# Windowed attention, LayerNorm and a ReLU MLP on one core: from wanted times for a list scheduler to an order written down as a permutation

## The chip, the cores and the metric

One core of one Trainium2 chip runs the whole program in one launch. The metric is the device time of an execution in microseconds (us), smaller is better. The engines are called as the profile calls them: PE (TensorE, matrix products and transposes), PEld (its weight loads), DVE (VectorE), ACT (ScalarE), POOL (GpSimd) and SP (SyncE, which issues every DMA of this kernel on one queue). Each engine works through its own list of instructions in order, and an instruction waits until what it reads is there and what it overwrites is done with.

## The reference

Four batches of eight heads, 768 positions, 64 channels. Each position attends to its neighbours less than 16 away and to 24 summaries of 32 positions each (the maximum of the block's keys, the mean of its values):

```python
k_sum = k.reshape(B, H, nb, block, D).max(axis=3)
v_sum = v.reshape(B, H, nb, block, D).mean(axis=3)
scores_l = where(|i - j| < 16, scale * q @ k.T, -1e9)
scores_s = scale * q @ k_sum.T + log(32)
a = softmax(concat(scores_l, scores_s))         # denominator + 1e-09
x = a @ concat(v, v_sum)                        # -> (B, S, 512)
xn = (x - mean) / sqrt(var + 1e-6) * g_ln       # LayerNorm
out = x + relu(xn @ w_ch1) @ w_ch2              # 512 -> 2048 -> 512
```

Inputs and output are float32.

## The kernel before, in words

The 3072 positions are 24 tiles T of 128, each with two halves of four heads (t = 2T, 2T+1). Two tiles form one of 12 groups of the MLP. Products run in float16 with a high and a low part (tiles `x16`, `w1`/`w2`, `qhl`, `kh`/`kl`, `h` with two parts), so that three products stand for one in float32.

- **Batch 0** (T = 0 to 5) takes a path of its own (`early_k`, `early_qk`, `softmax`, `early_transp`, `early_pv`) in float32, while the weights are loaded. `fetch_k0` loads keys `spare_x8` to `spare_x11`, `fetch_q` loads queries (`spare_x0` is the first), `fetch_v0` the values. `early_qk` computes scores `s`, `softmax` reads them with four DVE instructions (listed as ISA, in the profile as CUSTOM_DVE_ANT_0) into `p`, and these free the two banks that the next scores need.
- **Weights.** They come as 64-bit words into `raw` (four buffers); `merge_w` (L914) joins the halves on DVE into `m1_f` and `m2_f`, one TENSOR_SCALAR and two SCALAR_TENSOR_TENSOR for each of 32 chunks. `gram`, `scale_w1` and `split_w` (L949, L977) find scales and split the merged weights; `low` is the low part of a w1 chunk, computed on PE.
- **LayerNorm** (`ln`, L866) ends on DVE with the low half of `x16_T`, and `lnT` (L882) transposes it by a DMA (DMA_TRANSPOSE) into `xt_g`, which the first product of the MLP reads.
- **The MLP** of a group is eight steps `g1` (into banks `h`, relu on ACT and DVE) and eight steps of the second product: `g2` (L1122) into two accumulators `a{g}_0`, `a{g}_1` for groups 0 to 2, `g2_wide` for groups 3 to 11. After the last step of a `g2` group a DVE add takes the accumulator into `x`, and the bank becomes that of the next group.
- **Batches 1 to 3** go through `load_q` (L666: two DMAs into `qs`, ACT then DVE make `qhl`), `load_k`, `heads`, `late_softmax` (transposed by a DMA into `pt`), `load_v` and `late_out`.
- `gain` (L1142) loads `g_ln`, spreads it over 128 partitions on PE and finds its scale on DVE; `warm` (L1158) is 36 transposes on PE whose result nobody reads.

What sets the order: all these functions only record operations in a `Plan`. At the end, `issue` (L400) runs a list scheduler over the recorded operations. `record` (L246) has found what each must wait for, `cost` (L290), `port` (L330) and `waits` (L338) give it durations and latencies, and `schedule` (L342) lets each engine take, of the operations whose inputs are ready, the one whose wanted time in the table `ORDER` is the smallest. The operations are then issued in the order of the computed starts. Every recorded instruction carries the line of `issue`, L406 before and L162 after the change, so rows are told apart by their tiles.

Of the kernel before, what the change touches and what calls it, by code (L numbers as in the profile page):

```python
# [26 lines left out]
P = 128  # L27
# [14 lines left out]
XB = 6  # L42
# [20 lines left out]
    "tWTU`SF-0X*bA{r;}gNg)SuXWjPI*52Yz)U%**{&qykqrvhJ76Q;sd*C9wkkUxs~axmMv5tHMX7wwrf<C+`FJz7e+9W&G)UF^hY_nbVAWb&NOR_c"
    "qu#uwu_){GTggyAbb+xx6ae%l-pm>de62SBf!BJ%cY8len4tFXg-Uv9B@fu?GhXr&=@a4aVzS(QyQK=3D;}L+mh*Fy<|hw&#lUtb;wFitq5dg|E|"
    "}fCYT&*I>>rtTmVW@tKVe9PabZ42ipjzsG{tZ@Kpk_R)aP>?83hH(;BAEmn%_U3ec>+<TJPm>Pp48MB!6H2&|x_t$eR%UVbB%IU{m+u@({xsJb`U"
    ")jq!%zFuQ>9rz7oLIy)&ENhH*jJBxMquBItaE}nCUX4{wrysdwgc?PDiyI6XFgfMm`9oaGw$8YxVM#RGf!kFzVjF7m32=@yxr{QoqRFQwL)Tpvjj"
    "1-vB|!NzcIp(7ICP3l03kF)s$+;93PV3?%PES$I0bjUNMj2tZ$HWrrs0t$t1r2ko(BL1Y8mvE5^ywIa`^%kXuQ>m4a7n_+{7_k;@t}me^Qlhs3GH"
    "*sjb8HzhlP&$bL6P=U?Ic)=l>7gJY;B;AcQ09F$G*@KvSQE^WBi2dR>XE^@4n1T2!M$V>sF|HwVe~ka&zdbLB)Wi1l8H~9oRNxx#HSRf^`?1U7d%"
    "FW`Y~TeK7~syT9+JE7Q0jc_cdp?Y+-8B@bf=J5bMh*^5&N`H)-(2!e=r&&u0b*+$@}vv_9lM*lku;z?>%|t;&YcVv8lY@#@f^f=QQ>Yj^fMl@p|$"
    "R+$P~5=Tzp#zv*B8W9|#F8y@lQV~vHp6KBoeN%m~rRLnc!vq?NWcsvHC1Cl8Yf5iLq9lRcU=%4vqd}s2#-w{mB#vkxh5{!G~sRhT_d}plU8h^Xr@"  # L70
    "Xr3tn;8ghJ~~6BIt3^O|Ha80YXoa;!+w0{!IjQ-e18%9!cXz$<XmmmWlVy-I<1N}q#tA-_%%lSZ1x+kQMBI$OD5dq^Ga0bKKRJ|lxw4Tr+!!?xo^"
    "gQ^Rf1u|8H!E0}>Ehp!xI`Ue{tbG4<bPt<L<7k7D4{IExn?;)7@7S+2D#&gWJx##yi{4%ft}zveFDa5ZzS#vXFqe~<6r6%P!$dwIc?-X89Kl6_xZ"
    "<k><le9eDgS7S!%GIlC2){S9jT;~kDk^qZ7bHuPeMb1l8?3#`Z*YUUZ1w?%%emDjXrl`Tfx@mYh@jQOm$NcbJ{2J_m=abXeOK)CqYw}~p!et&Dlh"
    "Seg2_IYRAMUgliW~>q53sIz7q36K4<fM08H@a~zUSI7d<ZUln|0Y=a#wLrKKG?3GZ%U8pBfVLL2Maa#76Q1<{@9*Re2SxW*=?%47bO|ku!a;0S>("
    "r%={E#%*({&LncJi=-4JMW^ccdBme#<u8E&mi@9UEPV8a+aoF|>d8K)bJPxX08}-GS#r}unRs0DC5g#EI4m>AX&kQWaPju~rlYWkdW!eq=y)duL*"
    "NDMP#*=$GpVGH;Kl>NrWz0tF%nC{3bgs3=2Iexsg2OczOqpm2V{}M-Z3FuWmcwb2*zX~@fn1A$QGXlrx5%p`_QqCXFF9m=&Hc;R1Gx6Tz;0@hdlm"
    "Lv&AcCB%Wpa5ynw&pwix*@Wvo@XC@@kV6zhH*4U~Mjq6Uvgm%XmkRCvDTPdOFu$UK*`7iyFXcc(Aq`$0PX;PJ-1@~HE{AoflTDb!?q;;iLw_8IF@"
    "<SOHP;)>rA`*R9PPzkVO^6rAA0KW1xM!|rC|5Avl*gE3zR7g@|^2&b{Y-sF}3nm!$KE_9fS(n@i_A@u@`skZjSN8ZhHH?~`p~jXh$Sb2+Sgan{hR"
    "#dDfjVbAaP9Y}riIvx#wE2gMIQOOrcVxwoy5PBvHL0fvO2F)<a2x!z6LYa5BY)?cLMB1&&9Of1&^QL&lbzD<#ud9XU8fr$0N)QN5sIB!8(cWv3Wj"
    "!r?G|H+zp<VZsFR&V!d-;h2yzyu{Y-d@bY_3dBckSbB1FZwaxAvlC9LLeob;Jm92<ZFaG;h>pjL$JLA+mLv#6l=4yc78)3^7e7}ddRbo!;H;B1UZ"  # L80
    "SyqWBH%=8L9KV-_X5vTH_~7&1t%sS=KJ2P^AZ0302|3K=Wb%heSRgr+f6>8NnAL<)S8H~0T}SvvxjDjQ6o~-7@z*X_?1{Ew0^-)N#?qIfyg$kQ~$"
    "(X>Y0azaM)Lhxout3$uUpk9vx~8W&$|uRcy+GB_B<j(l~vMT+y1I>oE_1Q6C(5IJx<swT;t?n!*Ij7Cw_X?DaVOg2+$$%>O>P(Y*uyj>AX(F*LzD"
    "j6<J!)NOwnYoTjgcr%8ckVfD%VBI$4YXj!7iG$YgS#bA^=63!jzf64TlOHx(PHSG1SXqBzAGI(5W7bK0hptP&6~TOPF_U@ly^r?pc|S4N`a<X4aO"
    "`Q$-l%Z_deVL-EU|+*l^n|EqS%OTG4NaR{*W{r5t8js<&-_WsJ8+*HP(|k;L|jkDb5`6t?UJDm!SVh(O30t7?R`vhBwzRAN=8wGuE47>RwL8nuVl"
    "k-Mspv9h&Dp)<RobBO;QjjZIunj*LjMMOIz;OGwV|O747!ZziD|SzqV9)`0pw{Y8ZqZ@`+mpSY_S=M=Tvg9qc_&<(?tIqamqS`3P<Wv(B&PR&V^f"
    "9bBePtB_#a7g)zkWAT_SAE~ht2tf5vNc-lbNrWBa|t<%|LiC5)!)RlGV@Qv$8bxb?so$>_h2jh<j^;{t-=zYq5ENc!kX?C_yXT0Dtc+}cV1`#Pxl"
    ">YPE+>>&oe)`^e1rRNyL3N{vqdV_U9bWsZi^X+z6H|FdMwZp3on59p-M$8pJ60GpA%2pS5263jX^I8wr@b6f9CB?0v;o%w=wTX`?fOT^OTv#d(bR"
    "BvjCN$$zmAG=w!&71l^EBgW)tlKxf}X<bXK@ktUMO-%;d=fE}ax`8h(G)tV`z@;}Znb$y!n)D{do9yvM>><_xJ*Gizwa!OF@5-y*i^H<w>71H)Ls"
    "&i~{&D)zX7xgHTVK}M!Wuv2m3@uYrNrV9eD*?K)oCA=nH{;#oXM6UX+}OCr7k7$X##BP9x^r~EFNHSp207~-qHO5{FSP~{x^aP_{6D2Ty!r>ZaQG"
# [1237 lines left out]
```

## Time and profile before

| | us |
|---|---|
| median of three runs | 614.92 |
| lowest, highest | 613.8, 615.09 |
| the profiled execution's own time | 612.62 |
| its span in the trace | 610.8 |

The span is the part of the profiled execution that the trace covers; 1.82 us lie around it. The mean granted PE clock over the span is 0.990 of full speed.

| engine | busy us | share of the span |
|---|---|---|
| PE | 589.5 | 97% |
| DVE | 522.1 | 85% |
| ACT | 418.9 | 69% |
| POOL | 162.3 | 27% |

The shares are averages over stages with different limits. The program has a start-up until the first MLP product, a long stretch in which merging and splitting weights on DVE and ACT runs beside the first MLP groups, and from about 232 us a steady stage of late attention and wide MLP groups. So the views of most use are the busy time of each engine stage by stage, and, inside a stage, the timeline with what ended each wait. Busy time of PE is partly modelled: a matmul group that runs at half clock counts as busy for twice as long.

### The profile page before, as it was taken

What the parts mean: (1) busy time and instruction counts of PE and PEld (TensorE: products, weight loads), DVE (VectorE), ACT (ScalarE), POOL (GpSimd) and SP (SyncE); (2) the same over time, 40 slices, a digit from 0 to 9 for tenths busy, and PEclk for the clock granted to TensorE, in tenths of its full rate; (3) what the DMA queues carried; (4) which work ended last, traced back from release to release, by engine and by line L of the source; (5) the groups of instructions that cost most, each with busy time, mean ns of one, the idle gap of its engine ahead of it and who ended that gap; (6) DMA issues with size and microseconds to landing.
All of it is one profiled execution on the core that took longest, in us unless ns stands there. A gap on an engine that the chain in (4) does not pass through costs nothing.

```text
span 610.8 us, 16490 instructions
## 1 busy us (share of the span) xinstructions
PE 589.5 (97%) x6235; PEld 474.3 (78%) x6235; DVE 522.1 (85%) x1396; ACT 418.9 (69%) x1003; POOL 162.3 (27%) x261
## 2 busy tenths in 40 slices
PE   6988999999999899999999999999899999999997
PEld 5556778885444377888888888888788888888886
DVE  5798999999989999999899899599798896784471
ACT  4788886578677659977878777468758766543340
POOL 7131221211122333305253142303413323020201
PEclk8899999999999899999999999999999999999999
DMA  8988896443665735755857655326864443120000
GB/s 303 324 227 288 273 270 242 109 141 114 175 148 157 205 101 164 182 145 167 207 140 167 151 147 131 81 69 150 174 181 116 119 126 59 34 61 18 1 35 35
DMA packets 116262, 90.70 MB, mean 148 GB/s; under 512 B 69597, under 2 KB 100445, under 8 KB 116182
## 3 DMA queue, kind: packets, MB, share of 16 engines
q1 hardware_dynamic: 116182, 89.65, 54.3%
q8 instruction: 49, 0.80, 0.6%
q14 instruction: 31, 0.25, 0.1%
HBM read 67.05 MB, written 6.29 MB: 120 GB/s over the span
## 4 chain that ended last, share of the span: by engine, by line
PE 57%; DVE 17%; ACT 10%; DMA 10%; issue 5%; SPq 1%; POOL 1%; ACTq 0%; DVEq 0%; POOLq 0%
PE h L406 26%; PE acc_a L406 9%; PE acc_s L406 6%; PE acc_o L406 6%; ACT p L406 3%; DMA raw<-in_w 3%; DVE h_x L406 3%; DVE wide L406 3%; PE s L406 2%; DMA vst<-in_va 2%; PE o L406 2%; PE a L406 2%; DVE kl L406 1%; DVE m L406 1%; DVE x L406 1%
## 5 line engine op out<-in xcount | busy, mean ns | idle before, releaser
L406 PE MATMUL h<-xt,w_u 128*128 128x256 f16 x2304 | 266.4, 273 | 1.1 <-ACT wide L406 0.9
L406 PEld LDWEIGHTS <-w_u 128*128 128x128 f16 x2304 | 223.0, 98 | 29.8 <-issue 2.6
L406 PEld LDWEIGHTS <-h_x 128*128 128x128 f16 x1752 | 170.3, 98 | 48.6 <-issue 5.5
L406 DVE TENSOR_TENSOR wide<-wide 128x128 f32<-128x128 f32 (+1 forms) x224 | 79.3, 363 | 13.5 <-ACT wide L406 11.7
L406 DVE TENSOR_TENSOR h_x<-wide,h_x 128x896 f16<-128x896 f32 x72 | 78.0, 1089 | 12.7 <-ACT h_x L406 12.0
L406 ACT CAST h_x<-wide 128x896 f16<-128x896 f32 x72 | 66.8, 932 | 28.0 <-DVE wide L406 24.1
L406 ACT ACTIVATE p<-p,mn,sv 128x120 f32<-128x120 f32 x144 | 68.3, 476 | 13.3 <-POOL mn L406 13.3
L406 ACT ACTIVATE wide<-h 128x512 f32<-128x512 f32 x72 | 42.2, 591 | 44.5 <-PE h L406 34.0
L406 POOL TENSOR_TENSOR p<-p,p 128x480 f16<-128x480 f32 x36 | 43.7, 1214 | 94.2 <-ACT p L406 81.3
L406 PE MATMUL acc_o<-w,h_x 128*128 128x256 f16 x432 | 58.5, 273 | 0.0
L406 PE MATMUL a<-w,h_x 128*128 128x512 f16 x240 | 55.3, 387 | 2.9 <-DVE x L406 2.9
L406 POOL TENSOR_SCALAR mn<-mn,sv 128x4 f32<-128x4 f32 x36 | 23.5, 652 | 127.2 <-DVE mn L406 110.3
L406 ACT ACTIVATE bst<-bst 128x384 f32<-128x384 f32 (+2 forms) x55 | 32.3, 587 | 22.8 <-DMA bst<-in_qa 7.0
L406 PE MATMUL acc_a<-mix_x,h_x 128*128 128x256 f16 x324 | 45.0, 273 | 0.0
L406 PE MATMUL acc_s<-mix_x,h_x 128*128 128x256 f16 x324 | 43.9, 273 | 0.0
L406 DVE SCALAR_TENSOR_TENSOR m<-raw,m 128x512 uint32<-128x512 uint32 x64 | 43.4, 683 | 0.3
L406 POOL TENSOR_TENSOR x<-x,uv 128x512 f32<-128x512 f32 x18 | 24.9, 1401 | 67.2 <-DVE uv L406 67.1
L406 DVE SCALAR_TENSOR_TENSOR kl<-ksg,sv,kh 128x640 f16<-128x640 f32 x36 | 32.7, 908 | 4.1 <-ACT kh L406 4.1
L406 PE MATMUL acc_a<-w,h_x 128*128 128x256 f16 x216 | 35.4, 273 | 0.0
L406 DVE CUSTOM_DVE_ANT_0 p<-s,mask 128x120 f32<-128x120 f32 x144 | 35.0, 273 | 0.1
L406 DVE SCALAR_TENSOR_TENSOR qhl<-qs,sv,qhl 64x512 f16<-64x512 f32 x36 | 28.5, 792 | 7.4 <-ACT qhl L406 6.5
L406 ACT ACTIVATE qhl<-qs,sv 128x512 f16<-128x512 f32 x36 | 25.7, 714 | 11.0 <-DMA qs<-in_qt 9.6
(136 smaller groups left out, 913.4 us busy)
## 6 DMA issues: line engine op xcount, KB each, us to landing
raw<-in_w SPq DMA_DIRECT2D x32, 512.0 KB
ksg<-in_kt SPq DMA_DIRECT2D x36, 368.0 KB
qs<-in_qt SPq DMA_DIRECT2D x72, 128.0 KB
out_x<-x SPq DMA_DIRECT2D x24, 256.0 KB
bst<-in_ks SPq DMA_DIRECT2D x20, 192.0 KB
bst<-in_qa SPq DMA_DIRECT2D x15, 256.0 KB
bst<-in_vs SPq DMA_DIRECT2D x20, 192.0 KB
vst<-in_va SPq DMA_DIRECT2D x36, 96.0 KB
```

The costliest lines, as they stand in the source:

```text
L406: getattr(getattr(nc, self.ops[i].engine), op)(*a, **k)
```

## The change

`Plan` loses everything that computed an order: dependences, costs, latencies and the list scheduler. `ORDER` now is a permutation of the recorded operations, and `issue` plays it. The operations are the same, engine by engine (11701 instructions on PE, 1398 on DVE, 747 on ACT, 266 on POOL, 460 on SP as listed); tiles, buffers and banks are the same; only the order on each engine differs. The core of the diff, one line of the table each:

```diff
-    "c-n263EWKO`~R<5o=2M;l`Y9pDN7h3Ny|ZmQWMz{CdpFbP|=1{%F?2dic()kdx${`B_`S_$DW8|t8aylR36VP_wRkrJimY6@BjbzdX0JJ%(?ITy0"
...
+    "c-k#k37n4g8a>ZD#%y-N5N-@13|%4-GSpQlOQGzQM2swDN!F5mEGZ;g3E3`15-LK-nq;zFD*HYdGw*Zm`R3l={O0?<cl$5TbDnd~^WKj?Sqg=4fw"
...
     def record(self, engine, op, a, k):
-        on_chip = lambda x: isinstance(x, bass.AP) and x.space != bass.MemoryType.DRAM
...
-            self.ops.append(x)
-        x.after.pop(i, None)
+        if not self.joined:
+            self.ops.append((engine, []))
+        self.ops[-1][1].append((op, a, k))
         if self.joined is None:
             self.joined = True
...
-    def schedule(self, rank, after):
...
     def issue(self, nc):
-        wanted = np.cumsum(np.frombuffer(zlib.decompress(base64.b85decode(ORDER)), "<i4"))
-        self.start, self.end = self.schedule(1.0 * wanted, [self.waits(x) for x in self.ops])
-        self.time = max(self.end)
-        for _, i in sorted(zip(self.start, range(len(self.ops)))):
-            for op, a, k in self.ops[i].calls:
-                getattr(getattr(nc, self.ops[i].engine), op)(*a, **k)
+        order = np.cumsum(np.frombuffer(zlib.decompress(base64.b85decode(ORDER)), "<i2").astype(int))
+        for i in order:
+            engine, calls = self.ops[i]
+            for op, a, k in calls:
+                getattr(getattr(nc, engine), op)(*a, **k)
```

Three places show what moved.

**The start.** SP's first loads before, up to the first query tile (`spare_x0`); `raw1_1` is the first weight chunk, `xn1` the row that receives `g_ln`:

```order
L406 DMA spare_x8_82<-in_ks 128x768
L406 DMA spare_x9_83<-in_ks 128x768
L406 DMA spare_x10_84<-in_ks 128x768
L406 DMA raw1_1_227<-in_w1 128x4x256
L406 DMA xn1_97<-in_g_ln 1x512
L406 DMA spare_x0_86<-in_qe 128x512
```

and after:

```order
L162 DMA spare_x8_82<-in_ks 128x768
L162 DMA xn1_97<-in_g_ln 1x512
L162 DMA spare_x10_84<-in_ks 128x768
L162 DMA spare_x11_85<-in_ks 128x768
L162 DMA vend_92<-in_vb 32x2x256
L162 DMA spare_x9_83<-in_ks 128x768
L162 DMA spare_x1_89<-in_va 128x2x256
L162 DMA raw1_1_227<-in_w1 128x4x256
L162 DMA spare_x0_86<-in_qe 128x512
```

`g_ln`, the fourth key tile `spare_x11`, a block of values `vend` and the first value tile `spare_x1` now stand ahead of the first query tile. The loads up to it were 1.97 MB and are 2.69 MB, 0.72 MB more. On PE, `gain` now precedes the 36 filler transposes; on DVE, the reduction of `gain` with its scales and all four key maxima precede the first `p`, where before three key maxima did.

DVE's list up to the low half of `x16_1`, which the first transposed tile waits for; before:

```order
L406 SCALAR_TENSOR_TENSOR xn3_144<-x1_132,mv1_142,gb_65 128x512
L406 ISA p2_81,mn5_157<-s5_1_156,spare_x7_94 128x128
L406 ISA mn5_157 128x1
L406 ISA p2_81,mn5_157<-s5_1_156,spare_x7_94 128x128
L406 ISA mn5_157 128x1
L406 TENSOR_SCALAR m1_7_240<-raw1_7_239 128x512
L406 ISA p2_81,mn5_157<-s5_0_155,spare_x7_94 128x128
L406 ISA mn5_157 128x1
L406 SCALAR_TENSOR_TENSOR m1_7_240<-raw1_7_239,m1_7_240 128x512
L406 SCALAR_TENSOR_TENSOR x16_1_145<-xn3_144,rs1_143,x16_1_145 128x512
```

and after:

```order
L162 SCALAR_TENSOR_TENSOR xn3_144<-x1_132,mv1_142,gb_65 128x512
L162 SCALAR_TENSOR_TENSOR x16_0_122<-xn2_121,rs0_120,x16_0_122 128x512
L162 ISA p2_81,mn5_157<-s5_1_156,spare_x7_94 128x128
L162 ISA mn5_157 128x1
L162 TENSOR_SCALAR m1_4_234<-raw1_4_233 128x512
L162 SCALAR_TENSOR_TENSOR x16_1_145<-xn3_144,rs1_143,x16_1_145 128x512
```

Ahead of `x16_1` stand 24 merge instructions before (9 TENSOR_SCALAR and 15 SCALAR_TENSOR_TENSOR on `m1` tiles) and 16 after (6 and 10); one key reduction more stands there. All else ahead of it is the same in kind and number. The eight merge instructions come later, beside the MLP's first groups.

**The second and third MLP group.** PE's list where group 1's second accumulator `a1_1` is finished and its bank is taken over by `a2_1` (products of group 1's and group 2's relu outputs `h14`, `h16`, `h22` with chunks of w2); before:

```order
L406 MATMUL a1_1_372<-w2_15_343,h14_x5_381 128x512
L406 LDWEIGHTS h14_x5_381
L406 MATMUL a1_1_372<-w2_15_343,h14_x5_381 128x512
L406 LDWEIGHTS h16_x6_425
L406 MATMUL a2_1_427<-w2_0_328,h16_x6_425 128x512
```

and after, with the last five of six products into `a2_0`:

```order
L162 LDWEIGHTS h22_x9_436
L162 MATMUL a2_0_426<-w2_14_342,h22_x9_436 128x512
L162 LDWEIGHTS h22_x9_436
L162 MATMUL a2_0_426<-w2_14_342,h22_x9_436 128x512
L162 LDWEIGHTS h22_x9_436
L162 MATMUL a2_0_426<-w2_15_343,h22_x9_436 128x512
L162 LDWEIGHTS h22_x9_436
L162 MATMUL a2_0_426<-w2_15_343,h22_x9_436 128x512
L162 LDWEIGHTS h22_x9_436
L162 MATMUL a2_0_426<-w2_15_343,h22_x9_436 128x512
L162 LDWEIGHTS h16_x6_425
L162 MATMUL a2_1_427<-w2_0_328,h16_x6_425 128x512
```

Six products into the other accumulator `a2_0` now stand between the two, one `LDWEIGHTS` with each. The DVE add `x3<-a1_1` that frees the bank moves among its neighbours too.

**Late queries.** SP's list around the two halves of `qs114`, the queries of t = 40, and the LayerNorm transpose of T = 16; before:

```order
L406 DMA_TRANSPOSE pt0_345<-p16_344 128x8x128
L406 DMA qs114_929<-in_qt 64x512
L406 DMA_TRANSPOSE xt_8_885<-x16_16_884 128x8x128
L406 DMA qs114_929<-in_qt 64x512
L406 DMA ksg41_934<-in_kt 128x2x368
L406 DMA_TRANSPOSE pt1_349<-p16_344 128x8x128
```

and after:

```order
L162 DMA vst1_69<-in_va 96x256
L162 DMA qs114_929<-in_qt 64x512
L162 DMA vst1_69<-in_va 64x256
L162 DMA qs114_929<-in_qt 64x512
L162 DMA_TRANSPOSE xt_8_885<-x16_16_884 128x8x128
L162 DMA ksg41_934<-in_kt 128x2x368
L162 DMA vst1_69<-vsum3_783 24x128 x2
```

Both halves of the queries now stand ahead of the transpose `xt_8`, which waits for `x16_16`; before, the second half stood behind it.

## Rows read from the trace of the kernel before

**Rows 1.** The page's list of busy time by engine.

```profile
PE 589.5 (97%) x6235; PEld 474.3 (78%) x6235; DVE 522.1 (85%) x1396; ACT 418.9 (69%) x1003; POOL 162.3 (27%) x261
```

**Rows 2.** Table by stretch: from:to, length, PE PEld DVE ACT POOL busy, PEclk, DMA, GB/s.

```profile
0.00:12.08 12.08, 7.76 (x55) 6.41 (x55) 5.85 (x11) 3.69 (x11) 9.46 (x48) 1.00 0.84 287
12.09:18.90 6.81, 6.30 (x44) 3.94 (x45) 6.71 (x36) 5.54 (x24) 2.34 (x10) 0.50 1.04 358
18.92:40.89 21.97, 20.66 (x197) 11.50 (x196) 18.01 (x66) 17.77 (x55) 5.35 (x17) 1.00 0.96 278
40.89:58.00 17.11, 15.09 (x151) 10.43 (x153) 15.52 (x48) 13.87 (x43) 2.20 (x8) 1.00 0.91 279
58.00:140.00 82.00, 81.33 (x828) 66.47 (x826) 77.81 (x210) 62.64 (x174) 16.97 (x33) 1.00 0.68 203
140.00:200.00 60.00, 58.53 (x457) 28.61 (x456) 56.65 (x147) 46.17 (x118) 13.81 (x18) 1.00 0.59 155
203.23:206.64 3.41, 3.04 (x8) 1.08 (x8) 3.35 (x6) 0.72 (x2) 0.45 (x1) 0.50 0.76 208
200.00:232.00 32.00, 27.65 (x229) 19.58 (x227) 30.97 (x80) 20.13 (x41) 10.55 (x12) 0.95 0.53 138
232.00:424.00 192.00, 191.35 (x2288) 167.62 (x2286) 175.40 (x473) 148.62 (x344) 58.71 (x71) 1.00 0.58 147
424.00:460.00 36.00, 33.77 (x432) 29.58 (x430) 32.08 (x98) 26.36 (x61) 12.30 (x15) 1.00 0.71 171
460.00:610.00 150.00, 147.00 (x1573) 130.15 (x1571) 103.05 (x236) 74.10 (x141) 30.64 (x31) 1.00 0.24 61
```

**Rows 3.** Timeline, start-up: start, us, engine, line, operation, tiles, count, [idle before <-releaser].

```profile
1.85 5.79 PE L406 MATMUL warm<-ident 128*128 128x128 f32 x36 [1.85 <-POOL ident masks.py:199]
...
10.87 0.29 DVE L406 CUSTOM_DVE_ANT_0 p<-s,spare_x 128x128 f32<-128x128 f32 x1
...
21.61 0.29 DVE L406 CUSTOM_DVE_ANT_0 p<-s,spare_x 128x128 f32<-128x128 f32 x1 [2.10 <-PE s L406]
...
27.38 0.29 DVE L406 TENSOR_REDUCE scales<-gram 128x1 f32<-128x128 f32 x1 [0.91 <-PE gram L406]
...
40.14 0.75 DVE L406 SCALAR_TENSOR_TENSOR x<-xn,rs,x 128x512 f16<-128x512 f32 x1 [0.73 <-ACT x L406]
...
40.92 1.25 SPq L406 DMA_TRANSPOSE xt<-x  x1
...
43.70 1.48 PE L406 MATMUL h<-xt,w_u 128*128 128x256 f16 x12 [0.20 <-DMA xt<-x]
```

**Rows 4.** Groups of instructions: weight merges on DVE (busy us, mean ns).

```profile
L406 DVE SCALAR_TENSOR_TENSOR m<-raw,m 128x512 uint32<-128x512 uint32 x64 | 43.4, 683 | 0.3
L406 DVE TENSOR_SCALAR m<-raw 128x512 uint32<-128x512 uint32 x32 | 13.2, 416 | 1.9 <-DMA raw<-in_w 1.9
```

**Rows 5.** Timeline about 200 us, PE and the DVE add it waits for.

```profile
199.66 1.03 PE L406 MATMUL a<-w,h_x 128*128 128x512 f16 x4
...
202.81 0.74 DVE L406 SCALAR_TENSOR_TENSOR x<-a,scales,x 128x512 f32<-128x512 f32 x1
...
203.60 9.41 PE L406 MATMUL a<-w,h_x 128*128 128x512 f16 x36 [2.91 <-DVE x L406]
```

**Rows 6.** Timeline about 434 us: SP, ACT and PE for the queries.

```profile
429.27 1.07 SPq L406 DMA_DIRECT2D qs<-in_qt  x1
...
430.44 1.26 SPq L406 DMA_TRANSPOSE xt<-x  x1
...
431.75 0.59 SPq L406 DMA_DIRECT2D qs<-in_qt  x1
...
434.59 0.72 ACT L406 ACTIVATE qhl<-qs,sv 128x512 f16<-128x512 f32 x1 [1.35 <-DMA qs<-in_qt]
...
436.15 0.24 PE L406 MATMUL s<-kh,qhl 128*64 128x120 f16 x2 [1.40 <-DVE qhl L406]
```

More of the change, by code (lines that the diff above doesn't have):

```diff
@@ L1 @@
 import base64
-import heapq
 import math
@@ L5 @@
 from contextlib import ExitStack, contextmanager
-from types import SimpleNamespace
 import numpy as np
@@ L63 @@
[L63 to L77, printed above, removed]
@@ L156 @@
+    "?g+>}Lg9jsT29&cHxyT3$71P<sOp&?nurw|S<9BnSlTSPn@raTAWr$}hD}n`cI;!%@!T+Kfxn{_d!?BhAze-bg6Va@=oV7(pxGf|V%gMoA;Wbfc3"
+    "v-mpb3X6ptdWeoLHjT1-}Dm"
 )
@@ L210, in step @@
     def step(self, f):
[L213 to L237 removed]
+        return f
+    def tile(self, pool, shape, dt, tag, name, bufs=1):
+        return pool.tile(shape, dt, tag=tag, name=name, bufs=bufs)
     @contextmanager
@@ L267, in record @@
-        busy, moving, tail = self.cost(engine, op, a, k, ins, outs)
-        columns = 0
-        if engine == "tensor":
-            columns = ({'matmul': 4, 'transpose': 2}[op] if ins[-1].dtype == F32 else 1) * math.prod(n for _, n in a[0].ap[1:]) * ins[0].ap[0][1] / P
-            columns /= 1 + (a[0].ap[0][1] == D)
-        if self.joined:
-            x = self.ops[i]
-            x.calls.append((op, a, k))
-            x.after.update(after)
-            x.busy += busy
-            x.columns += columns
-        else:
-            rows = ins[0].ap[0][1] if ins else 0
-            half = engine == "tensor" and (
-                (3 if rows > D else 4) if a[0].ap[0][1] == D else 1 if rows == D else 2 * (ins[-1].dtype in (F16, BF16))
-            )
-            busy += 40 * (half == 3) + 60 * (half == 4)
-            x = SimpleNamespace(engine=engine, calls=[(op, a, k)], after=after, busy=busy, moving=moving, tail=tail, columns=columns, stage=self.stage, port=self.port(engine, op, ins, outs), half=half)
-            self.ops.append(x)
@@ L329, in port @@
-    @staticmethod
-    def port(engine, op, ins, outs):
-        on_sbuf = [x for x in ins if x.space != bass.MemoryType.PSUM]
-        if engine == "gpsimd":
-            return len(on_sbuf) > 0
-        wide = [x for x in on_sbuf if math.prod(n for _, n in x.ap[1:]) > 8]
-        return engine == "vector" and (len(wide) > 1 or op == "tensor_scalar" and ins[0].space != bass.MemoryType.PSUM)
-    def waits(self, x):
-        e = [self.ops[j].engine for j in x.after]
-        return [(j, self.SAME[a] * y if a == x.engine else self.WAIT[a] or self.ops[j].tail) for a, (j, y) in zip(e, x.after.items())]
```

291 lines of the change are left out of this document (52 added, 239 removed).

## The prediction, made before the changed kernel was run

> **What bounds the kernel now.** I read the list of busy time first: PE works 97% of the span, DVE 85% [rows 1]. Together they say little, since no average tells which engine ends a wait. So next the table by stretch [rows 2]. From 232 to 424 us PE is busy 191.35 of 192.00 us: PE is the bound, and no order can gain there more than 0.65 us. From 58 to 140 us the gap is 0.67, from 460 to 610 us it is 3.00 with the end of the program in it. What an order could win lies elsewhere: 4.32 us before 12.08, 1.31 from 18.92 to 40.89, 2.02 from 40.89 to 58, 1.47 from 140 to 200, 4.35 from 200 to 232 and 2.23 from 424 to 460 us. Besides, two stretches run at a granted clock of 0.50, that is at 1.2 GHz: 12.09 to 18.90 with 6.30 us busy, and 203.23 to 206.64 with 3.04 us busy. At 2.4 GHz their work would take half, so they cost up to 3.1 and 1.5 us.
>
> In the same rows DVE is close to full over the whole front part: from 12.09 to 232 us it is busy 205.7 us of 219.9 (the sum of six rows, without the one that lies inside 200 to 232), so 14.2 us are idle. A fill of PE's gaps must therefore come from DVE work placed better, not only from PE work. The DMA engines too are nearly full until 58 us, a share of 0.84 to 1.04.
>
> Third, the timeline of the stretches with gaps. In the start-up, DVE waits 2.10 us for scores at 21.61, 0.91 for a gram at 27.38 and 0.73 for ACT at 40.14; the last ends the LayerNorm that the first transposed tile (40.92) and the first MLP product (43.70) hang on [rows 3]. At 200 us PE has finished `a1_1` and waits 2.91 us, until DVE's add at 202.81 has freed the bank; it is right behind this wait that the clock is at half [rows 2, 5]. At 434 us the second half of the queries is issued at 431.75, behind a LayerNorm transpose at 430.44, while the first half was issued at 429.27; ACT then waits 1.35 us for the load and PE 1.40 us for `qhl` [rows 6].
>
> **The change part by part.** No instruction is added or removed, so every term is a wait that goes, shrinks or comes.
>
> *Start-up, until 58 us.* Eight merge instructions leave the way to `x16_1`: 5 x 0.683 + 3 x 0.416 = 4.66 us of DVE work [rows 4]. They aren't saved; they come later in a DVE list that has idle time of 82.00 - 77.81 = 4.19 us from 58 to 140 and 3.35 from 140 to 200 [rows 2]. On the other side stand the longer loads ahead of the first query. They are 0.72 MB more, which at the 358 and 287 GB/s of the first two rows is 2.0 to 2.5 us [rows 2]. This time isn't lost if DVE uses it: the gain's reduction, its scales and a fourth key maximum now stand ahead of the first `p` (10.87 before), where DVE has worked only 5.85 of 12.08 us [rows 2, 3]. What can go are the three DVE waits, 2.10 + 0.91 + 0.73 = 3.74 us, and PE's 2.02 us of gaps behind the first MLP product. The bounds are 0 and -5.8. I take half of each, -1.9 - 1.0 = -2.9: the deferred 4.66 us is larger than the waits, but the scores' wait of 2.10 is one on PE's chain, not on the order of merges, and the full DMA engines set their own floor.
>
> A second thing is moved here: the 36 filler transposes (1.85, 5.79 us long [rows 3]) stand behind `gain`, which waits for `g_ln`. Nobody reads them, and what they do is keep PE busy ahead of the scores. They will start later and end nearer to the first scores. In the trace of before the clock fell to half at 12.09 although PE had just worked; where it falls now no row shows. I count it at nothing for the forecast, since DVE is busy 6.71 of 6.81 us in this stretch and so would hold a faster PE, and keep its 3.1 us for a rival.
>
> *140 to 232 us.* Six products into `a2_0` come between `a1_1` and `a2_1`. Four such products took 1.03 us [rows 5], so six are about 1.5 us, and the wait of 2.91 shrinks to some 1.4 us if the add comes at the same time. That time is set by DVE, which is busy 30.97 of 32.00 and 56.65 of 60.00 us [rows 2]. If DVE stays as it is, the six products are only moved. The most that DVE can give back in the two stretches is its idle time, 3.35 + 1.03 = 4.38 us; the most that PE can is its gaps and the half clock, 1.47 + 4.35 + 1.5 = 7.3 us. I take half of the smaller, -2.2, with bounds of 0 and -7.3.
>
> *424 to 460 us.* Both query halves go out ahead of the LayerNorm transpose. The second half was issued 2.48 us behind the first (431.75 - 429.27); with one value load between them that is about one issue slot, 0.59 to 1.07 us [rows 6]. So `qhl` comes some 1.4 us earlier at the least, which is the whole of PE's wait of 1.40. The transpose moves back by one load, 0.59 us; its reader, the MLP product of group 8, isn't waited for at this place in the rows. The term is -1.4, with bounds of 0 (the next wait is as late) and -2.2 (all gaps of the stretch go).
>
> *New waits.* Every other instruction also stands in a new neighbourhood, and over 14,000 of them cannot be followed one by one. In the order, the distance between a producer and its reader is mostly longer after 232 us, and shorter by 0.2 to 1.3 us at about ten places (scores of t = 17, 19 and 37, relu outputs of groups 9 to 11). No row shows these. The nearest are stretches without a marked stall, with gaps of 0.65 and 0.67 us; the largest gap of any stretch is 4.35 [rows 2]. So I take +1.0, with bounds of 0 and +4.
>
> The sum is -2.9 - 2.2 - 1.4 + 1.0 = -5.5 us. The profiled execution took 612.62 us, 610.8 of it in the span, so it would take 607.1. The median of the runs shown is 614.92, 2.3 us above the profiled one. The forecast stands on that median: 609.4 us.
>
> **The rivals.**
>
> *DVE is the bound, and the gain stays away.* For it: 205.7 of 219.9 us busy, and the deferred merges have to be done before group 0 can be finished. Against it: 14.2 us are idle, and the waits named are on PE's and ACT's chains, which a reorder can hide. Then the first two terms are nothing, and -1.4 + 1.0 leave 614.5 us, no change.
>
> *The first query comes too late.* Its place is the first `p` on DVE, 10.87 us before. With 0.72 MB more ahead of it, it moves by up to 2.5 us. If the merges and maxima placed ahead of it don't fill this time (they need loads too, from a DMA that is full), the whole front part, which DVE bounds, is shifted by it, and the eight deferred merges are a debt on top that takes up the idle time elsewhere. It decides from a first `p` at 13.4 on. For it: the DMA share of 0.84 to 1.04 [rows 2]. Against it: DVE had 6.23 us idle before 12.08, and some 2 us of its work are drawn into this time. The time is 2.5 - 1.4 + 1.0 = +2.1, 617.0 us, slower.
>
> *The clock holds too.* Both stretches at 0.50 go. By the rows, the second began right behind the wait of 2.91 us, and six products now stand in it; the first began behind a start-up in which PE was busy 7.76 of 12.08 us, and the fillers now stand closer to the scores. The mechanism is worth up to 3.1 + 1.5 = 4.6 us beyond the sum, which makes 604.8 us. Against it: DVE is busy 6.71 of 6.81 and 3.35 of 3.41 us in exactly these stretches, so a faster PE would wait for DVE; and a stall of 1.4 us may be left at the second. The Trainium skill, "TensorE: Matmul & The Clock Gate", section "HAM oscillation — how this bites in real kernels", describes the same mechanism: gaps between bursts of products let the chip halve TensorE's clock, and each next burst pays for it. The trace of before agrees at 203.23 us, behind the gap of 2.91 us; by that rule, closing the gap gives back more than the gap.
>
> **How the numbers follow.** The forecast gets 0.58, the clock rival 0.20, the DVE rival 0.11 and the late query 0.11. The range goes from 603.0, below the clock rival at 604.8, since the bounds of the three terms add up to more than the forecast takes, to 615.2, above the DVE rival; the slower rival stays outside. Within the likeliest case I expect 606.5 to 612.5. Differences of 0.2%, 1.2 us, are about what a measurement of this kernel can tell. Faster by more than that hold the forecast and the clock rival, 0.78; no change the DVE rival, 0.11; slower the late query, 0.11.
>
> **What would show it.** In the profile of the changed kernel: the first `p` at 11 to 13 us, with DVE's share before it above 5.85 of 12.08; the low half of `x16_1` before 40.14 and the first MLP product before 43.70, by 1 to 4 us; PE's wait ahead of `a2_1` under 1.5 us, and its clock there; no wait of PE for `qhl` at t = 40; between 232 and 424 us gaps below 2 us. The prediction is wrong if the first MLP product is not earlier, or if it is earlier and the lead is gone at 232 us because DVE catches up with its merges there, or if PE's gaps behind 232 us exceed 4 us.

## The result, and the profile after

The new kernel takes 607.38 us (median of four runs, 606.57 to 609.29), the old one 614.36 us (four runs, 612.73 to 615.09). The ratio is 0.9895 with a 95% interval of 0.9863 to 0.9926: 7.0 us or 1.1% faster. The profiled executions compare as 605.4 to 610.8 us of span, 5.4 us. The forecast was 5.5 us faster. The sum came out; the table by stretch shows that its terms did not come out with it.

Busy time by stretch after (columns as in [rows 2], the last row is the rest of the span):

```profile
0.00:12.08 12.08, 8.01 (x39) 6.52 (x39) 5.64 (x12) 3.15 (x7) 8.93 (x45) 1.00 0.84 275
12.09:18.90 6.81, 6.75 (x71) 3.60 (x73) 5.46 (x32) 5.23 (x25) 2.55 (x15) 1.00 1.08 387
18.92:40.89 21.97, 21.46 (x246) 13.41 (x247) 21.69 (x80) 19.84 (x66) 6.34 (x18) 1.00 0.93 258
40.89:58.00 17.11, 17.11 (x178) 13.00 (x177) 17.08 (x63) 16.81 (x60) 4.25 (x9) 1.00 1.01 327
58.00:140.00 82.00, 81.99 (x781) 64.09 (x780) 79.93 (x209) 63.15 (x160) 17.44 (x33) 1.00 0.72 207
140.00:200.00 60.00, 57.59 (x446) 28.67 (x444) 58.87 (x144) 45.50 (x118) 16.54 (x21) 1.00 0.64 161
200.00:232.00 32.00, 30.83 (x348) 24.55 (x347) 30.89 (x90) 25.11 (x57) 7.10 (x11) 1.00 0.63 153
232.00:424.00 192.00, 185.13 (x2208) 162.80 (x2207) 178.30 (x458) 143.87 (x326) 60.65 (x68) 1.00 0.55 141
424.00:460.00 36.00, 35.61 (x448) 31.12 (x447) 32.07 (x90) 25.30 (x57) 11.86 (x13) 1.00 0.68 160
460.00:605.00 145.00, 141.27 (x1500) 125.04 (x1494) 101.73 (x230) 70.43 (x136) 30.71 (x32) 1.00 0.26 62
```

PE does the same work in both, so its lead is the difference of the work done up to a time. What ran at a clock of 0.50 in [rows 2] counts half: 3.15 of 6.30 us, and 1.52 less of the stretch from 200 us. By the rows the new kernel has done 53.3 us at 58 us and the old one 46.7, a lead of 6.7.

That is 1.3 us too much. The two traces hold no record of the granted clock before 5.25 us (old) and 10.18 us (new), and a row reads 1.00 where there is no record; but the products there were slow. The two of `gain`, which took 2.04 us in the new kernel (below), took this in the old one:

```profile
8.68 1.12 PE L406 MATMUL gain<-xn,ones 1*128 1x512 f32 x2 [1.03 <-DMA xn<-in_g_ln]
```

`gain` and the fillers together were busy for 8.19 us after and for 6.91 before, for the same work. So the lead at 58 us is 5.4. The rows up to 232 us add 4.4: 9.8 us ahead. From 232 to 424 us PE now has gaps of 6.87 us, before 0.65 [rows 2], and the lead falls to 3.6. From 424 to 460 it gains 1.8, and the 5.4 us then reached are what the spans show at the end. The change won 9.8 us, nearly twice what it shows, and gave 6.2 of them back. (Leads of 6.7 and 11.1 us in the expectations below are by the rows alone.)

Timeline after, the start-up rows that answer to [rows 3]:

```profile
4.07 2.04 PE L162 MATMUL gain<-xn,ones 1*128 1x512 f32 x2 [4.07 <-POOL msk L162]
6.04 6.15 PE L162 MATMUL warm<-ident 128*128 128x128 f32 x36
...
13.12 0.28 DVE L162 CUSTOM_DVE_ANT_0 p<-s,spare_x 128x128 f32<-128x128 f32 x1
...
34.29 2.71 SPq L162 DMA_TRANSPOSE xt<-x  x2
...
34.73 0.75 DVE L162 SCALAR_TENSOR_TENSOR x<-xn,rs,x 128x512 f16<-128x512 f32 x1
```

The first `p` comes 2.25 us later than before (13.12 against 10.87 [rows 3]), and yet the low half of `x16_1` comes 5.4 us earlier (34.73 against 40.14) and the first MLP product 3.6 us earlier (40.07 against 43.70). The second transpose on SP follows it, and ahead of 58 us neither PE nor DVE has a wait of over 1 us left, but for the first one.

Timeline after at group 2's second accumulator, which answers to [rows 5]:

```profile
195.01 9.22 PE L162 MATMUL a<-w,h_x 128*128 128x512 f16 x42 [1.60 <-DVE x L162]
```

The wait is 1.60 us where the forecast said 1.4, and the clock stays full: it is 1.00 from 193 to 204.3 us.

Timeline after for the queries of t = 40, which answers to [rows 6]:

```profile
422.74 0.59 SPq L162 DMA_DIRECT2D qs<-in_qt  x1
423.43 2.35 SPq L162 DMA_TRANSPOSE xt<-x  x1
...
428.11 0.75 DVE L162 SCALAR_TENSOR_TENSOR qhl<-qs,sv,qhl 64x512 f16<-64x512 f32 x1
...
430.32 0.24 PE L162 MATMUL s<-kh,qhl 128*64 128x120 f16 x2
```

The second half of the queries stands ahead of the transpose, `qhl` is ready at 428.9, and PE reads it 1.5 us later without a wait. Where PE waits now, its timeline from 232 to 424 us shows; the two longest, and the longest for ACT (a third, 1.00 us at 391.19, is for DVE's add again):

```profile
257.51 0.24 PE L162 MATMUL s<-kh,qhl 128*64 128x120 f16 x2 [2.10 <-DVE mn L162]
...
273.32 0.82 PE L162 MATMUL acc_s<-mix_y,h_x 128*128 128x256 f16 x6 [1.82 <-DVE x L162]
...
306.82 9.33 PE L162 MATMUL h<-xt,w_u 128*128 128x256 f16 x84 [0.89 <-ACT wide L162]
```

The bank for the scores of t = 25 is still being read by DVE, an accumulator waits for DVE's add, a relu for ACT: PE is ahead of both engines at these places.

### The profile page after: what moved, and what is told of

Read it like the earlier page. It is cut to its first block, busy times and chain, and to the rows that moved or that the text cites. A ratio compares the mean times of both kernels' runs of the same rounds, so it can differ in the third digit from the quotient of the medians.

```text
span 605.4 us, 16480 instructions
## 1 busy us (share of the span) xinstructions
PE 585.8 (97%) x6235; PEld 472.8 (78%) x6235; DVE 531.7 (88%) x1396; ACT 418.4 (69%) x1003; POOL 166.4 (27%) x261
## 4 chain that ended last, share of the span: by engine, by line
PE 28%; DVE 15%; DMA 5%; ACT 4%; issue 3%; POOL 1%; SPq 1%; DVEq 0%; ACTq 0%
PE h L162 12%; PE acc_a L162 6%; PE acc_o L162 4%; PE acc_s L162 4%; DVE wide L162 3%; DVE h_x L162 3%; DVE x L162 2%; DVE kl L162 2%; DMA vst<-in_va 1%; DMA ksg<-in_kt 1%; ACT h_x L162 1%; DVE qhl L162 1%; DVE v L162 1%; DMA bst<-in_qa 1%; DVE p L162 1%
## 5 line engine op out<-in xcount | busy, mean ns | idle before, releaser
L162 DVE TENSOR_TENSOR h_x<-wide,h_x 128x896 f16<-128x896 f32 x72 | 79.1, 1105 | 17.5 <-ACT h_x L162 17.1
L162 DVE TENSOR_TENSOR wide<-wide 128x128 f32<-128x128 f32 (+1 forms) x224 | 83.6, 388 | 6.1 <-ACT wide L162 3.9
L162 POOL TENSOR_TENSOR p<-p,p 128x480 f16<-128x480 f32 x36 | 48.1, 1337 | 133.4 <-ACT p L162 124.9
L162 PE MATMUL a<-w,h_x 128*128 128x512 f16 x240 | 53.6, 379 | 1.6 <-DVE x L162 1.6
L162 POOL TENSOR_SCALAR mn<-mn,sv 128x4 f32<-128x4 f32 x36 | 20.8, 579 | 69.1 <-DVE mn L162 56.5
L162 POOL TENSOR_SCALAR rs<-mv 128x1 f32<-128x1 f32 x24 | 13.7, 572 | 82.3 <-DVE mv L162 76.9
```

Source lines behind the costliest of these rows:

```text
L162: getattr(getattr(nc, engine), op)(*a, **k)
```

## The experiments

Each experiment is a play of the same 3168 recorded operations in another order; one leaves out 35 fillers, no other leaves out anything. Where two orders are joined, a prefix is taken from one (every operation that its trace starts before a time, with all it depends on) and what is left follows in the order of the other.

### a58_b: the new start, the old rest

```diff
-ORDER = new
+ORDER = [what new starts before 54.5 us, in new's order] + [the rest, in old's order]
```

> The new order for every operation that it starts in its first 54.5 us (435 of 3168), then what is left in the old order. At 58 us the new kernel had done 6.7 us more PE work and 3.8 us more DVE work than the old one. Theory (DVE is the bound of the front part, so its lead is what stays): about 3.8 us below the old kernel, 610.6. Rival (PE's lead at 58 us is the whole gain): about 607.4, as the new kernel. Rival (the old order from there on stalls where the new one doesn't): 613 to 614.4.

Measured 612.12 us against 613.59, ratio 0.9977 (0.9951 to 1.0003). Rows of this kernel:

```profile
58.00:140.00 82.00, 78.25 (x752) 62.41 (x751) 77.89 (x204) 60.47 (x161) 13.99 (x24) 1.00 0.70 198
...
200.00:232.00 32.00, 26.98 (x269) 20.22 (x268) 29.85 (x79) 20.24 (x45) 6.23 (x11) 1.00 0.54 129
```

PE's lead at 58 us is there, 5.7 us by the same count (`gain` and the fillers took 7.83 us here), but the old order spends 3.75 us of gaps from 58 to 140 us, and at 232 us 1.9 us are left. Between the first theory (3.8 us kept) and no gain: about 2 us in the spans, and the interval doesn't exclude zero. PE's lead alone is not the gain.

### a232_b and b232_a: which half has the late waits

```diff
+a232_b: ORDER = [what new starts before 222 us] + [the rest, in old's order]
+b232_a: ORDER = [what old starts before 232 us] + [the rest, in new's order]
```

> The new order for every operation that it starts in its first 222 us, then the rest in the old order. At 232 us the new kernel is 11.1 us ahead in PE work and 8.0 us in DVE work, and gives 6.2 us of PE's lead back before 424 us. Theory (the give-back is DVE's backlog, no matter in which order): the lead left is DVE's, 8.0 us, 606.4. Rival (the give-back is made by the new order behind 232 us itself): nearly the whole 11.1 us stay, 603.3.

> The old order for every operation that it starts in its first 232 us, then the rest in the new order. Theory (backlog): no lead to give back, so the new order behind 232 us costs nothing and saves the wait for late queries, 612.5 to 614. Rival (the new order behind 232 us has waits of its own): 6.2 us of waits less 1.8 saved, about 618 to 619.

a232_b takes 605.73 us (ratio 0.9854, 0.9813 to 0.9896), b232_a 622.5 us (1.0131, 1.0089 to 1.0173). The row of a232_b behind 290 us:

```profile
290.00:424.00 134.00, 134.00 (x1596) 118.44 (x1594) 117.75 (x317) 102.44 (x231) 38.76 (x43) 1.00 0.56 135
```

and of b232_a:

```profile
232.00:290.00 58.00, 51.33 (x634) 43.02 (x632) 52.39 (x134) 40.28 (x97) 16.06 (x19) 1.00 0.51 138
290.00:424.00 134.00, 130.35 (x1524) 114.63 (x1524) 121.31 (x310) 99.81 (x225) 43.64 (x49) 1.00 0.56 137
```

The times alone don't part a232_b's theories (606.4 or 603.3), but the rows do. From 290 to 424 us the old order has no gap at all although PE came there early, and the new order has 3.65 us of gaps although it came without a lead. So the new order's late part has waits of its own behind 290 us, with a lead or without. Between 232 and 290 us this is less clear: b232_a has waits of 2.3 us for the scores' bank and 1.8 us for the accumulator there, much like the 2.10 and 1.82 of the new kernel, but the join leaves its DVE some 8 us of work that the new order had done by then, so a backlog isn't excluded. That b232_a loses more than the 618 to 619 expected has another part: 6.67 us of gaps from 232 to 290, right behind the seam, where two orders meet that had not done the same operations. Against a58_b (612.12 us, taken at the same time), a232_b also shows what the new order is worth between 54.5 and 222 us: 6.4 us by the medians.

### a_warm and a_fill1: the fillers and the clock

```diff
 PE, a_warm:
+warm (36 transposes)
 gain
-warm (36 transposes)
 s0 ...
```

> The new order with one operation moved: the 36 filler transposes on PE back ahead of the spread of the gain, as in the old kernel. Theory (the fillers' later place is what held the granted clock at full from 12 to 19 us): the clock falls to 0.50 at about 12 us for some 6.8 us again and the time rises by 1.5 to 3 us, 609 to 610.4. Rival (the clock is held by the closer packed products, or DVE hides the slower PE): 607.4 with no change beyond 1 us.

```diff
-WARM = 36
+WARM = 1
```

> The new order with one filler transpose in place of 36 (nothing of the result is left out, nobody reads the fillers). With the fillers ahead of the gain the whole gain was lost, but there the gain's product also ended 3.6 us later and ACT, which had to scale by it first, delivered the first keys 3 us late. Theory (the clock is what the fillers' place is worth): PE idles from 6 to 12 us, the clock is at 0.50 for some microseconds behind 12 us, and the time rises by 1.5 to 3 us, to 609 to 610.4. Rival (what costs is only the gain queued behind the fillers): 607.4, whatever the clock does.

a_warm takes 613.74 us, 0.9995 (0.9975 to 1.0015): one operation moved, and the whole gain is gone, twice what the clock theory allowed. a_fill1 takes 607.98 us, 0.9897 (0.9866 to 0.9929): nothing is lost without the fillers. The start of a_warm on PE:

```profile
2.34 6.32 PE L160 MATMUL warm<-ident 128*128 128x128 f32 x36 [2.34 <-POOL ident masks.py:199]
8.59 1.12 PE L160 MATMUL gain<-xn,ones 1*128 1x512 f32 x2
...
12.93 0.45 PE L160 MATMUL s<-spare_x,spare_x 64*64 64x128 f32 x8 [2.96 <-ACT spare_x L160]
```

on its ACT:

```profile
11.95 0.69 ACT L160 ACTIVATE gb<-gain,scales 128x512 f32<-128x512 f32 x1 [4.28 <-DVE scales L160]
```

with its table by stretch:

```profile
12.09:18.90 6.81, 4.74 (x36) 2.09 (x37) 5.21 (x15) 3.12 (x13) 2.57 (x10) 0.62 1.08 387
```

and of a_fill1, the timeline of PE:

```profile
11.26 1.13 PE L162 MATMUL s<-spare_x,spare_x 64*64 64x128 f32 x16 [4.46 <-DMA spare_x<-in_qe]
12.32 2.06 PE L162 MATMUL v<-spare_x,blk 128*120 128x512 f32 x2
...
18.12 0.67 PE L162 MATMUL s<-spare_x,spare_x 64*64 64x128 f32 x16
18.72 1.12 PE L162 MATMUL v<-spare_x,blk 128*120 128x512 f32 x2
```

with its table by stretch:

```profile
12.09:18.90 6.81, 6.81 (x51) 3.21 (x44) 3.75 (x22) 4.34 (x21) 1.76 (x8) 1.00 1.08 387
```

The clock theory is right on the clock and wrong on its price. In a_warm the clock is at 0.50 from 13.66 to 20.48 us, the 6.8 us foretold. In a_fill1 the row reads 1.00, but the first record of the clock in this trace is at 17.51 us, and the products show half speed until about then: the same 16 score products take 1.13 us at 11.26 and 0.67 at 18.12, the same two products into `v` 2.06 and 1.12. So PE ran at half speed through the first scores. Although they began 1.0 us earlier, with no fillers ahead (11.26 against 12.23), the first MLP product came 1.5 us later than in the new kernel (41.57 against 40.07); and yet the time is only 0.6 us longer, less than either kernel's runs differ among themselves. What the fillers' place does is keep the clock up at the start: it is 1.00 from 12.09 to 18.90 us in all eight traces with the fillers between `gain` and the scores, and 0.50, 0.62, 0.63, 0.75 and 0.75 in the five with the fillers first. a_fill1 speaks against the clock being worth much of the 7 us.

What a_warm pays is a chain across three engines: behind the fillers `gain` ends at 9.7 instead of 6.1 us; DVE, whose list begins with the reduction of `gain`, starts that much later with it and with the key maxima; ACT has the scaling `gb` in its list ahead of the copies of the first keys, waits 4.28 us for the scale, and PE waits 2.96 us for the keys. The first `p` comes at 16.45 us, 3.3 later than in the new kernel. In the old kernel `gain` had been as late (8.68 us), but nothing that the first scores need stood behind it on ACT.

### a_merge, b_merge, a_merge_sp: the eight merges

```diff
 DVE, a_merge (b_merge is the reverse, in the old order):
 ... x16_0
+m1_4 (2), m1_9 (2), m1_6 (2), m1_7 (2)
 x16_1
-the same eight, among the instructions behind it
```

> The new order with the eight merge instructions put back ahead of the low half of x16_1 on DVE, all else as it is. Theory (deferring them is worth most of the start-up's gain): the first MLP product comes up to 4.7 us later, and since loads queued behind the transposes of x16_1 feed these merges and others, PE's lead at 58 us falls by 2 to 5 us; 609 to 612. Rival (DVE is the bound and must do them anyway): 607 to 608.4.

> The old order with one thing of the new done alone: the same eight merge instructions moved behind the low half of x16_1 on DVE. Theory (the merges held back x16_1, with it the transposes on SP, and behind these the next weight loads): x16_1 and the first MLP product come 3 to 4 us earlier, the DVE wait of 1.33 us for a raw load at 47.7 us goes, PE's lead at 58 us is 1 to 3 us, and 1 to 2.5 us of it last: 611 to 612.5. Rival (it needs the new order of the loads and key maxima too): 613 to 614.4.

a_merge takes 614.47 us, 1.0015 (0.9986 to 1.0044): the gain is gone, and 2.5 us more than the theory allowed. b_merge takes 620.83 us, 1.0104 (1.0075 to 1.0134): the same edit alone, done to the old order, costs 6.7 us where 2 were to be won. SP in a_merge:

```profile
33.84 7.10 SPq L160 DMA_TRANSPOSE xt<-x  x2
...
41.76 1.16 SPq L160 DMA_DIRECT2D raw<-in_w  x1
```

its DVE:

```profile
38.93 0.75 DVE L160 SCALAR_TENSOR_TENSOR x<-xn,rs,x 128x512 f16<-128x512 f32 x1
...
46.81 0.43 DVE L160 TENSOR_SCALAR m<-raw 128x512 uint32<-128x512 uint32 x1 [3.55 <-DMA raw<-in_w]
```

and SP in b_merge:

```profile
34.34 0.34 SPq L160 DMA_DIRECT2D qs<-in_ks  x1
42.59 0.38 SPq L160 DMA_DIRECT2D raw<-in_w  x1
```

with b_merge's DVE:

```profile
40.48 0.75 DVE L160 SCALAR_TENSOR_TENSOR x<-xn,rs,x 128x512 f16<-128x512 f32 x1 [1.61 <-ACT x L160]
```

In a_merge `x16_1` comes 4.2 us later than in the new kernel (38.93 against 34.73), SP stands 7.10 us at the two transposes instead of 2.71, and the weight loads listed behind them start 3.9 us later (41.76 against 37.87 in the new kernel's trace); DVE then waits 3.55 us for a weight. In b_merge it is the other way round: the old SP list has a weight load ahead of the transposes. This load needs one of four raw buffers, the buffer is emptied by a merge that now stands behind `x16_1`, and SP issues nothing from 34.7 to 42.6 us. Nor does `x16_1` come earlier (40.48 against 40.14 [rows 3]); in the old order the eight merges had filled time in which DVE waited for ACT anyway. So the deferral seems to pay only together with SP's list, which has the weight loads behind the transposes; this is argued from the two traces, as the old order with both edits was not run. To test that this list is what counts, a_merge with two of the loads moved back ahead:

```diff
 SP, a_merge_sp (all else as a_merge):
 xt_0 <- x16_0
+raw1_8, raw1_11 <- in_w1
 xt_0 <- x16_1
-raw1_8, raw1_11, among the loads behind it
```

> The new order with the eight merges put back ahead of x16_1, which cost the whole gain, and on SP the next two weight loads moved ahead of the second LayerNorm transpose that waits for x16_1. Theory (what cost was SP standing at this transpose with the weight loads behind it): the DVE wait of 3.55 us for a weight at 46.8 us shrinks below 1 us and at least half of the loss comes back: 608 to 611. Rival (what cost is the later first MLP product itself): 613 to 614.5.

Measured 617.33 us, 1.0047 (1.0024 to 1.0071): worse, not better. SP, PE and DVE in this kernel:

```profile
35.62 4.83 SPq L160 DMA_DIRECT2D raw<-in_w  x2
40.54 1.24 SPq L160 DMA_TRANSPOSE xt<-x  x1
```

```profile
47.09 5.28 PE L160 MATMUL h<-xt,w_u 128*128 128x256 f16 x24 [5.97 <-DMA xt<-x]
```

```profile
52.62 0.16 DVE L160 TENSOR_SCALAR scales<-gram 128x1 f32<-128x1 f32 x1 [9.26 <-PE gram L160]
```

The time is outside both ranges. DVE has no wait for a weight any more, so this part of the theory held; but the transposed tile, issued at 40.54 us behind two loads of 0.5 MB, is now read at 47.09, after a wait of PE of 5.97 us. The late product then holds DVE too: a `gram` that DVE needs stands behind it on PE, and DVE waits 9.26 us for it. PE's clock is at 0.50 from 42.51 to 52.75 us besides (in b_merge from 48.01 to 58.25), so part of the loss can be the clock; no run parts the two. The loss in a_merge is thus not the weight loads alone: as long as `x16_1` is late, either the weights or the tile are late on SP, and the rival, the later first MLP product, is the nearer reading. Over the kernels with the new late order, the time mostly goes up with the start of that product: 607.38 us with it at 40.07, 607.98 at 41.57 (a_fill1), 614.47 at 44.10 (a_merge), 613.74 at 45.15 (a_warm), 617.33 at 47.09.

### a_two: two waits taken out by hand

```diff
 DVE: p<-s24 (third)
+p<-s24 (fourth; 7 others stood between)
 ...
 x6 <- acc3_s1
+x7 <- acc3_s1 (3 others stood between)
```

> The new order with two DVE instructions moved: the fourth score reduction of t = 24 directly behind the third (it stood 7 instructions later, and PE waited 2.10 us for it at 257 us), and the add of the third accumulator to x7 directly behind that to x6 (PE waited 1.82 us for it at 273 us). Theory (the new order behind 232 us makes these waits itself): both waits shrink, 2.10 to 0 and 1.82 to 0.4, and the time falls by up to 3.5 us, to about 604. Rival (DVE's backlog): PE waits the same time at other places, 607.4.

Measured 607.2 us, 0.9893 (0.9859 to 0.9927): no change against the new kernel. Three of PE's four longest waits in its trace from 232 to 424 us (the fourth is 1.49 us at 394.11, for a DVE add):

```profile
256.99 0.57 PE L160 MATMUL o<-v,pt 128*64 128x64 f16 x24 [1.30 <-DVE x L160]
271.26 0.81 PE L160 MATMUL acc_s<-mix_y,h_x 128*128 128x256 f16 x6 [1.11 <-DVE x L160]
...
307.18 11.00 PE L160 MATMUL h<-xt,w_u 128*128 128x256 f16 x84 [2.05 <-ACT wide L160]
```

The wait for the scores' bank is gone, and PE waits at the next reader of DVE's work instead, and at 307 us longer than before. (The trace is of a run of 609.66 us, 2.5 above the median, and the 84 products at 307 us took 11.00 us in it, 9.33 in the new kernel's: behind the wait of 2.05 us the clock was at half.) The time is the rival's: single moves don't bring the lead back. That DVE is behind as a whole is not shown by this: it is busy 55.9 of 58 us from 232 to 290 here, and 56.42 in the old kernel, whose gaps there are 0.65 us.

### a_q and b_q: the late queries

```diff
 SP, a_q (b_q is the reverse, in the old order):
 qs114 (first half)
-qs114 (second half)
 xt_8 <- x16_16
+qs114 (second half)
```

> The new order with the second half of the queries of t = 40 put back behind the LayerNorm transpose on SP. Theory (this was the wait of 1.40 us at 434 us): PE waits 1.0 to 1.5 us for these queries again, 608.6. Rival (PE comes to this place 5.8 us earlier now, and DVE or ACT is what it waits for): the wait is larger than 1.5 us, or none, and the time moves by less than 0.5 us or by more than 2.

> The old order with both query halves of t = 40 ahead of the LayerNorm transpose on SP, alone. Theory (this order on SP made PE's wait of 1.40 us at 436 us): the wait goes and the time falls by about 1.4 us, to 612. Rival (the queries are late for another reason, since in the new order the swap back made no wait): the wait stays above 0.7 us and the time within 0.7 us of the old kernel.

a_q: 608.61 us, 0.9912 (0.9879 to 0.9946), within the spread of the new kernel. b_q: 612.09 us, 0.9981 (0.9959 to 1.0002). PE at these scores in a_q (no wait), then in b_q:

```profile
433.07 0.24 PE L160 MATMUL s<-kh,qhl 128*64 128x120 f16 x2
```

```profile
434.21 0.24 PE L160 MATMUL s<-kh,qhl 128*64 128x120 f16 x2 [0.51 <-DVE qhl L160]
438.23 7.04 PE L160 MATMUL h<-xt,w_u 128*128 128x256 f16 x63 [0.60 <-DMA xt<-x]
```

In the old order the swap takes 0.9 of the 1.40 us [rows 6], and 0.60 come back at the next product, for the transpose that moved behind; the time can't tell this from no change. In the new order, putting the load back makes no wait for the queries at all: there they are issued early enough against PE, in either order. The wait went, but the edit named was not what took it away there; what did, no run shows.

### a245_b_q: the new order to 245 us, the old one behind it

```diff
+ORDER = [what new starts before 245 us] + [the rest, in old's order]
 SP: qs114 (first half)
+qs114 (second half)
 xt_8 <- x16_16
```

> A candidate to beat both: the new order for every operation that it starts in its first 245 us, the old order for the rest, and both query halves of t = 40 ahead of the transpose. With the cut at 222 us the old rest had no wait at all from 290 to 424 us, but 3.5 us of waits at the seam, 229 to 234 us. Theory (the new order's rest has 3 to 5 us of waits of its own behind 290 us, the old one none): the seam's waits shrink, PE's lead of 11 us is kept for the most part, 603 to 604.5. Rival (DVE's backlog takes the lead back in any order): 606 to 607.5.

Measured 603.65 us (602.26 to 607.26) against 614.16, ratio 0.984 (0.9811 to 0.9869). By the medians this is 3.7 us below the new kernel, in runs taken at another time, and the intervals of the two ratios just overlap, so that it is faster than the old kernel is shown, and that it is faster than the new one is only likely. Its rows:

```profile
232.00:290.00 58.00, 54.85 (x639) 47.59 (x637) 53.00 (x147) 43.12 (x100) 17.42 (x26) 0.97 0.66 165
290.00:424.00 134.00, 134.00 (x1595) 118.42 (x1593) 120.17 (x321) 100.74 (x229) 40.21 (x44) 1.00 0.58 134
```

From 232 to 290 us it still loses 3 us, in which its clock is also at half for 3.4 us, and from 290 to 424 nothing. Over all runs, the kernels with the old order there have 0.00 to 0.06 us of gaps from 290 to 424 us, those with the new order 2.7 to 5.1.

## Why the prediction was right, and where only its sum was

The direction was right, and the total too (5.5 us forecast, 5.4 in the spans, 7.0 in the medians; 607.38 us lies within 606.5 to 612.5). The total was right by luck: three terms were too small by 4.5 us together, 0.7 us came where no term stood, and the fourth was too small by 5.2 the other way. One of the prediction's own signs of being wrong came true, gaps of PE behind 232 us above 4 us (6.87 from 232 to 424). The terms one by one:

- **Start-up, -2.9.** Measured: a lead of 5.4 us at 58 us, just within the bounds of 0 and -5.8. The waits went nearly as a whole, not by half: of DVE's 3.74 us 1.3 are left, for scores, and from 40.89 us PE is busy 17.11 of 17.11 us, DVE 17.08. The step that eight deferred merges shorten the way to `x16_1` is shown for the new order (a_merge), but the arithmetic was too simple: in the old order the same edit brings nothing and blocks SP (b_merge). What pays is, by the traces, the merges, the raw buffers and the place of the weight loads on SP taken together, and that `gain` stays ahead of the fillers: a_warm lost as much as a_merge. The bound left out the clock, which I had priced at nothing. Of the lead, 3.15 us stand against the half clock of this one trace of before; other traces with the old start had 0.75 there (b232_a, b_q) and 0.63 (b_merge).
- **140 to 232 us, -2.2.** Measured -3.8, within the bounds (another -0.7 came from 58 to 140 us, where no term stood). The wait ahead of `a2_1` shrank to 1.60 us as worked out, just above the 1.5 that was named as a sign; the half clock went, worth 1.5, and PE's gaps from 140 to 232 us fell from 5.82 [rows 2] to 3.58 us.
- **424 to 460 us, -1.4.** Measured -1.8 in the stretch, but a_q shows that the swap on SP isn't its cause in the new order, and b_q that it is worth at most 0.9 of the 1.40 us in the old one.
- **New waits, +1.0.** Measured +6.2 from 232 to 424 us, beyond the bound of 4, and nothing behind 460. This is the step that failed: I took the gaps of a stretch in which PE was the bound as a measure of what a new order would have there. What the runs show instead: behind 290 us the new late order has gaps of its own, 2.72 us in this trace and 3.65 without a lead (b232_a), where the old order has none even with one (a232_b, a245_b_q). The other 3.5 us fall between 232 and 290 us, where PE waits for DVE; a245_b_q, with the old order from 245 us on, loses about as much there, and what makes these waits stays open.

Of the rivals, the late first query is excluded as a loss: it did come 2.25 us later, short of the 13.4 us from which it was to decide by 0.3 (and past the 13 that was named as a sign), and DVE had used the time for the key maxima and the gain. That DVE is the bound was wrong for the front and half right behind 232 us: a_two shows waits that only wander, the kernels with the old late order that another order has none behind 290 us. What in the late order makes the difference is open; no run tells it apart. The clock rival saw both stretches at full clock, as it said, and at the start the fillers' place does it, as it also said. Its price was not borne out there: a_fill1, with PE at half speed through the first scores, took only 0.6 us longer. The time of 607.38 us, between 609.4 and 604.8, doesn't part it from the forecast.

## What to carry to other kernels

- A lead won in one stage is not safe in the next: 6.2 of 9.8 us went. Price "what is late next" for the new order and with the lead in place, and not from the gaps that the slower kernel had there.
- Two in-order lists that are tied by a few buffers (here DVE's merges and SP's loads over four raw buffers) should be reordered together. The same eight moves were worth 7 us in one list and cost 6.7 in the other.
- Orders can be cut and joined: prefix from one, rest from the other. Two such runs showed which half was worse, and a third gave a kernel 1.6% faster than the old one and by its median 3.7 us below the new.
- A sum that comes out proves none of its terms: count the work done up to the end of each stage, and check that the count closes at the end of the program.

## What the runs showed of the hardware that was not expected

The clock does not follow from a single gap. The old order's wait of 2.91 us ahead of `a2_1` was followed by a clock of 0.50 [rows 2, 5]. The same place in a58_b, and with nearly the same wait in its trace:

```profile
201.33 7.93 PE L160 MATMUL a<-w,h_x 128*128 128x512 f16 x36 [2.90 <-DVE x L160]
```

Here the 36 products took 7.93 us, not 9.41, and the stretch from 200 to 232 us has a clock of 1.00. Among the five traces with this wait (2.90 or 2.91 us), the clock fell behind it in two (before, b_q) and not in three (a58_b, b232_a, b_merge). In the start-up, the old order had 0.50 from 12.09 to 18.90 us in one trace, 0.63 in another and 0.75 in two. The Trainium skill, "TensorE: Matmul & The Clock Gate", section "HAM oscillation — how this bites in real kernels", describes a kernel in which longer waits between its bursts bring the clock down ahead of each next burst. The trace of before agrees at 203 us, already behind 2.91 us; a58_b kept its clock at the same wait. A term for the clock should have both prices in its range, and a_fill1 shows that half speed may leave little in the time.

At the start of a trace the shown clock is not evidence by itself. Up to the first record a row reads 1.00, while the same two products of `gain` took 2.04 us in the new kernel and 1.12 in the old one, and a_fill1's products ran at half speed to about 17.5 us. The duration of the same product at another time tells it.
